# Gate and value layer by seven products: sums moved to GpSimd, bit operations issued one by one, buffers placed elsewhere

## The chip, the cores and the metric

One core of one Trainium2 chip. The metric is device time in microseconds (us). TensorE is PE in the profile (its weight loads PEld), VectorE DVE, ScalarE ACT, GpSimd POOL, and SyncE, which issues nearly all DMAs, SP.

## The reference

```python
q_assign = argmax(norm(q) . norm(centroids)); k_assign = argmax(norm(k) . norm(centroids))
scores = where(q_assign == k_assign, q k^T / 8, -1e9)      # 2 batches, 8 heads, 768 x 64
x = concat_heads(softmax(scores) v)                        # 1536 x 512
h = sigmoid(x @ w_gate) * (x @ w_val)                      # 512 x 1536 each, float64 weights
y = h @ w_out                                              # 1536 x 512, float64
p = domain_probs / sum(domain_probs)
out = sum over 4 experts e of p[:, e] * (relu(y @ w1[e]) @ w2[e])     # 512 x 1024 x 512
```

## The kernel before, in words

Every fp32 operand of a matmul is split into a rounded high part and the low rest (ACT copies the high part, POOL or DVE subtracts), and each product is three matmuls: high-high, high-low, low-high. Work goes in three stages: attention; the gate, value and output layer (`moe1`); four experts (`moe2`).

**Attention** runs 96 items of 128 queries. Per item PE computes scores and transposes, DVE takes the row maximum (L430) and the low parts (L451), ACT the exponential and the high parts. The table `TAIL` hangs the first weights of `moe1` into the last 12 items.

**Weights** arrive as 64-bit words. Per half of a unit (256 rows by 256 columns of the gate or value matrix, one p) `magnitude` runs two operations on ACT, `bits` three on DVE (L632 to L634), `rounded` one on POOL (L638). Then `sums` (L668) makes four sums of blocks and `split` four slices of high (ACT, L676) and low part (POOL, L677). Output weights (`outer`, 128 rows) go the same way in one piece: magnitude, bits, round, `woh` (L730), `wol` (L731).

**`seven`** multiplies a 2 x 2 block of weights with a 2 x 2 block of X by seven products instead of eight, in the order 1, 6, 7, 5, 2, 4, 3, six matmuls each, in four PSUM banks: bank 0 holds product 1 and then 2, bank 1 product 6 and then 4, bank 2 product 7, bank 3 product 5 and then 3. ACT copies product 1 to `m1`, DVE adds u2 = m1 + P6 (L768), u3 = u2 + P7 (L772), bank 2 = u3 + P5 (L776, Pn being product n), bank 1 = u3 - P4 (L782), bank 3 = u2 + P3 (L786). `evict` empties a bank: for `gate` by a sigmoid on ACT (L822), for `value` by a product on DVE (L834), a copy on ACT (L835), a subtraction on POOL (L836). Entries of the list `work` are issued by `side()` after each product: side steps 0 to 5.

**`outp`** multiplies `h` with `woh` and `wol`: 48 matmuls in eight groups of six, each group first with the even `outer` (f = 0) and then with the odd one (f = 1), in four PSUM banks; DVE adds each group to `acc` (L857; for p = 0 a copy, L855). One `work` entry follows each group.

**Order.** Every queue runs in the order of the code, arranged by hand. For p = 1 to 5 a period is gate(p, 0), outp(p-1, 1), value(p, 0), gate(p, 1), outp(p, 0), value(p, 1): 264 matmuls. The weights of the next unit are converted in `gate`, summed and split in `outp` and `value`; the odd `outer` is converted in gate(p, 1). For p = 0 the order is gate(0, 0), value(0, 0), outp(0, 0), gate(0, 1), value(0, 1), while the sums t1 to t4 of X for batch 1 (`right_operands`) and their seven splits are made. `raw` has two buffers, `rwo` one. At the end the operands of `moe2` for batch 0 are built (`operands`) beside outp(5, 1), and `hidden(0)`, `hidden(1)` are the first two `seven` calls of `moe2`.

Of the kernel before, what the change touches and what calls it, by code (L numbers as in the profile page):

```python
# [75 lines left out]
class Net:  # L76
# [459 lines left out]
    def attention(self):  # L536
# [146 lines left out]
    def unit(self, p, which):  # L683
# [108 lines left out]
    def moe1(self, xadd, xscale):  # L792
# [94 lines left out]
        def weights(u):  # L887
            return [[u["sums"]]] + [[go] for go in u["split"]]

        def dense(steps, n):  # L890
            out = [[] for _ in range(n)]
            for i, gos in enumerate(steps):
                out[i * n // len(steps)] += gos
            return out
# [5 lines left out]
        split0(1, nc.vector)  # L900
        split0(6, nc.gpsimd)
        gate(0, 0, [[vs[0], o0["mag"]], [lambda: split0(2, nc.vector), vs[1], o0["bits"]], [vs[2], o0["round"], o1["load"]],
                    [vs[3], o0["split"], sums["t1"]], [o1["mag"]], [o1["bits"], xadd, xscale]])
        for go in load(U[1][0]):
            go()
        value(0, 0, [[sums["t2"]], [o1["round"], sums["t3"]], [o1["split"], sums["t4"]],
                     [lambda: split(4, nc.vector)], [lambda: split(0, nc.vector)]])
        outp(0, 0, [[lambda: split(5, nc.vector)], [lambda: split(3, nc.gpsimd)], [lambda: split(1, nc.vector)],
                    [lambda: split(6, nc.gpsimd)], [lambda: split(2, nc.vector)]], soon=True)
        gate(0, 1, conv(U[1][0], 0) + conv(U[1][0], 1))  # L910
        value(0, 1, [load(U[1][1])] + weights(U[1][0]))
# [260 lines left out]
```

## Time and profile before

| | |
|---|---|
| median of 3 runs | 1133.11 us (1130.19 to 1134.36) |
| profiled execution | 1131.03 us, span 1129.2 us, mean granted clock 0.976 |
| busy, share of span | PE 1054.1 us (93%), DVE 859.4 (76%), POOL 597.6 (53%), ACT 541.1 (48%) |
| attention | up to 277.2 us |
| `moe1` | 277.2 to 609.9 us |
| end of `moe1`, start of `moe2` | 609.9 to 644 us |
| rest of `moe2` | 644 to 1129.2 us |

The profile tells, per engine, what was busy and what ended each wait. A granted clock of 1.00 is 2.4 GHz, 0.5 is 1.2 GHz.

### The profile page before, as it was taken

To read this page: it belongs to the slowest core of one execution; us is meant where nothing else is said; L and a number is where in the kernel's file an instruction comes from. 1 tells how busy PE (TensorE), PEld (TensorE's weight loads), DVE (VectorE), ACT (ScalarE), POOL (GpSimd) and SP (SyncE) were. 2 spreads that over 40 slices of the span, in tenths; PEclk is the share of its full clock that TensorE was granted. 3 is DMA by queue.
4 is the path that set the end of the run, shared out by engine and by line. 5 is a ranking of instruction groups with operands and counts; after the bars stand their busy time and mean duration, and the time that the engine had idled before them with its cause. 6 is when DMAs were issued, how large, how long until landed. Compare 5 with 4: busy or idle time off the path is not lost.

```text
span 1129.2 us, 16200 instructions
## 1 busy us (share of the span) xinstructions
PE 1054.1 (93%) x5813; PEld 976.1 (86%) x5813; DVE 859.4 (76%) x1472; ACT 541.1 (48%) x1138; POOL 597.6 (53%) x519
## 2 busy tenths in 40 slices
PE   6999999997688898988989799999999999999998
PEld 6998999996588898888979799889998989998897
DVE  6998889897777677867766787777668877667765
ACT  4887888886444343434333443333334333333330
POOL 7566567766446455545454664444445454444430
PEclk8999999999799899999999899999999999999999
DMA  7667787643111111112110212222112422122201
GB/s 169 144 161 163 158 175 158 144 123 99 56 56 57 57 56 57 56 56 73 57 45 33 75 61 71 75 75 76 63 49 63 143 75 75 42 71 76 75 19 57
DMA packets 86481, 95.87 MB, mean 85 GB/s; under 512 B 42720, under 2 KB 59456, under 8 KB 86400
## 3 DMA queue, kind: packets, MB, share of 16 engines
q1 hardware_dynamic: 85968, 94.77, 31.0%
q8 instruction: 46, 0.75, 0.3%
q14 instruction: 35, 0.29, 0.1%
q10 hardware_dynamic: 432, 0.06, 0.0%
HBM read 65.07 MB, written 3.19 MB: 60 GB/s over the span
## 4 chain that ended last, share of the span: by engine, by line
PE 48%; DVE 2%; issue 1%; POOL 1%; ACT 0%; POOLq 0%; DVEq 0%; ACTq 0%
PE ph L755 22%; PE po L1047 8%; PE po L1048 8%; PE po L1046 8%; DVE sf L668 1%; PE po L645 1%; PE po L643 1%; PE po L644 1%; POOL G L836 0%; DVE sg L834 0%; DVE acc L857 0%; DVE ph L782 0%; DVE h2l L1023 0%; POOL nq L969 0%; DVE ph L786 0%
## 5 line engine op out<-in xcount | busy, mean ns | idle before, releaser
L1003 POOL TENSOR_TENSOR wol<-r,woh 128x512 fp32r<-128x512 f32 x62 | 80.2, 1295 | 154.2 <-ACT woh L1002 154.1
L1053 DVE SCALAR_TENSOR_TENSOR acc<-po,pn,acc 128x512 f32<-128x512 f32 (+1 forms) x181 | 129.8, 742 | 36.2 <-PE po L1048 36.2
L677 POOL TENSOR_TENSOR w1l<-sf,w1h 128x512 fp32r<-128x512 f32 x88 | 114.7, 1319 | 67.9 <-ACT w1h L676 67.9
L1048 PE MATMUL po<-woh,h2l 128*128 128x512 f32 (+1 forms) x374 | 145.7, 389 | 0.0
L1047 PE MATMUL po<-wol,h2h 128*128 128x512 f32 (+1 forms) x374 | 145.6, 389 | 0.0
L1046 PE MATMUL po<-woh,h2h 128*128 128x512 f32 (+1 forms) x374 | 145.0, 388 | 0.0
L755 PE MATMUL ph<-h,w1h 128*128 128x384 f32 x336 | 116.3, 346 | 16.1 <-DVE ph L776 6.5
L1022 ACT ACTIVATE h2h<-ph 128x384 fp32r<-128x384 f32 x128 | 62.6, 490 | 113.8 <-PE ph L755 88.2
L755 PE MATMUL ph<-h,w1l 128*128 128x384 f32 x336 | 115.0, 342 | 0.3 <-POOL w1l L677 0.3
L755 PE MATMUL ph<-l,w1h 128*128 128x384 f32 x336 | 114.6, 341 | 0.0
L451 DVE TENSOR_TENSOR pl<-T,ph 128x384 fp32r<-128x384 f32 x192 | 97.4, 548 | 13.7 <-ACT ph L450 11.3
L676 ACT ACTIVATE w1h<-sf 128x512 fp32r<-128x512 f32 x88 | 55.6, 633 | 91.0 <-DVE sf L668 89.9
L1023 DVE SCALAR_TENSOR_TENSOR h2l<-ph,h2h 128x384 fp32r<-128x384 f32 x128 | 70.9, 554 | 36.0 <-ACT h2h L1022 32.8
L450 ACT ACTIVATE ph<-T 128x384 fp32r<-128x384 f32 x192 | 84.5, 493 | 19.4 <-PE T L447 18.9
L643 PE MATMUL po<-G,woh 128*128 128x384 f32 x192 | 70.6, 368 | 24.0 <-ACT woh L730 12.0
L430 DVE TENSOR_REDUCE nm<-S 128x1 f32<-128x768 f32 x96 | 91.0, 948 | 2.3 <-PE S L427 1.3
L427 PE MATMUL S<-R,L 80*128 80x384 f32 (+1 forms) x384 | 91.6, 361 | 0.3 <-ACT P L438 0.3
L447 PE MATMUL T<-ident,P 128*128 128x128 f32 x576 | 82.1, 276 | 8.3 <-DVE pl L451 7.9
L438 ACT ACTIVATE P<-S,nm 128x768 f32<-128x768 f32 x96 | 87.7, 914 | 3.1 <-DVE nm L430 3.1
L677 POOL TENSOR_TENSOR w1l<-r,w1h 128x512 fp32r<-128x512 f32 x64 | 68.0, 1065 | 36.8 <-ACT w1h L676 36.8
L755 PEld LDWEIGHTS ph<-h,w1h 128*128 128x128 f32 x336 | 64.5, 192 | 21.5 <-issue 5.6
L1048 PEld LDWEIGHTS po<-woh,h2l 128*128 128x128 f32 x374 | 70.2, 188 | 14.5
(260 smaller groups left out, 2860.9 us busy)
## 6 DMA issues: line engine op xcount, KB each, us to landing
r<-in_moe_w_dram SPq DMA_DIRECT2D x64, 512.0 KB, 3.7
L<-hiq SPq DMA_DIRECT2D x32, 192.0 KB, 5.0
R<-hik SPq DMA_DIRECT2D x32, 192.0 KB, 4.6
raw<-in_moe_w_gate_dram SPq DMA_DIRECT2D x12, 512.0 KB, 3.9
raw<-in_moe_w_val_dram SPq DMA_DIRECT2D x12, 512.0 KB, 3.8
rwo<-in_moe_w_out_dram SPq DMA_DIRECT2D x12, 512.0 KB, 4.5
nq<-in_q_dram SPq DMA_DIRECT2D x16, 192.0 KB, 3.8
nk<-in_k_dram SPq DMA_DIRECT2D x16, 192.0 KB, 3.9
```

The costliest lines, as they stand in the source:

```text
L427: nc.tensor.matmul(ps[:, a, 0:384], l[0:k, c], r[0:k, a * 384:a * 384 + 384], start=l is L1, stop=l is L2)
L430: nc.vector.tensor_reduce(nm, ps[:, :, 0:384], axis=AX.XY, op=ALU.max, negate=True)
L438: nc.scalar.activation(r2(pt), ps[:, :, 0:384], AF.Exp, bias=nm, scale=1.0, accum_out=P["sums"][:, i:i + 1])
L447: nc.tensor.transpose(ps[:, j, :], pt[:, c:c + 128], self.ident)
L450: nc.scalar.activation(hi, ps, AF.Copy)
L451: nc.vector.tensor_tensor(lo, ps, hi.bitcast(F32), op=ALU.subtract)
L677: nc.gpsimd.tensor_tensor(lo[:, sl], x, hi[:, sl].bitcast(F32), op=ALU.subtract)
L755: nc.tensor.matmul(ps, x[:, a, j], y[:, j], start=first and j == 0 and k == 0, stop=j == 1 and k == 2, skip_group_check=not first)
L1046: nc.tensor.matmul(ps, Hh[:, f, c], wh[:, dc], start=f == 0, stop=False)
L1047: nc.tensor.matmul(ps, Hh[:, f, c], wl[:, dc], start=False, stop=False)
L1048: nc.tensor.matmul(ps, Hl[:, f, c], wh[:, dc], start=False, stop=f == 1)
L1053: nc.vector.scalar_tensor_tensor(a, ps, pe, a, op0=ALU.mult, op1=ALU.add)
```

## The change

`TAIL` moves the first unit's steps one item earlier. A sigmoid of one element after the last items of attention loads the sigmoid's table there. `bits` becomes three separate steps, so that the lists of `moe1` put one DVE operation after each product. Sums of weights (in `moe1`) and of X (t1 to t4 of batch 1, and of batch 0 for `moe2`) go from DVE to POOL. With `early`, bank 2 is emptied straight behind the addition of P5. For p = 0 the copies to `acc` go from DVE to ACT. The odd `outer` is loaded behind outp(p-1, 1) and converted from side step 0 of gate(p, 1), the even one in outp(p-1, 1). The first odd `outer` takes a `raw` buffer, so on SP its load and one load of the next gate unit stand ahead of the last transfers of attention (rd, rb, the last A and W). The pools `qk`, `pp`, `sm` of attention are allocated first, and `tmp`, `wb` before `accp`, so `m1`, u2, u3 lie where scores' operands were, not on `U`.

```diff
 TAIL = {
-    "open": (-12, 2), "load00": (-12, 2), "load01": (-11, 0),
-    "mag00": (-9, 2), "bits00": (-8, 1), ... "bits01": (-7, 1), ... "sums0": (-6, 2),
+    "open": (-12, 0), "load00": (-12, 0), "load01": (-12, 0),
+    "mag00": (-10, 2), "bits00": (-9, 1), ... "bits01": (-8, 1), ... "sums0": (-7, 2),
...
         for _, g in pvs:
             list(g)
+            self.nc.scalar.activation(self.warm1, self.half[:, 0:1], AF.Sigmoid)
...
     def bits(self, raw, f):
+        return [lambda: ..., lambda: ..., lambda: ...]
...
     def seven(self, w, ops, temps, evict, work=(), early=False):
         nc.vector.tensor_tensor(p7, u3, p5, op=ALU.add)
+        if early:
+            evict(1, 1, p7)
+            side()
         product(2, p1, first=False)
         evict(0, 0, p1)
         side()
         p4 = bank(1)
         product(4, p4)
         nc.vector.tensor_tensor(p4, u3, p4, op=ALU.subtract)
-        evict(1, 1, p7)
+        if not early:
+            evict(1, 1, p7)
         side()
...
-        sums, split = self.right_operands(1, spare, temp, nc.vector)
+        sums, split = self.right_operands(1, spare, temp, nc.gpsimd)
...
                 if p == 0:
-                    nc.vector.tensor_copy(a, ps)
+                    nc.scalar.activation(a, ps, AF.Copy)
...
+        def conv(u, a=None):
+            args = () if a is None else (a,)
+            return [[lambda: u["mag"](*args)]] + [[lambda k=k: u["bits"](*args, (k,))] for k in range(3)] + \
+                [[lambda: u["round"](*args)]]
+        def total(u):
+            return [lambda: u["sums"](Q)]
...
+        value(0, 0, [[sums["t2"]], [go[0]] + d[0], d[1] + [sums["t3"]], d[2], d[3] + d[4], [sums["t4"], o1["split"]],
+                     [lambda: split(0, V), go[1]]])
...
         for p in range(1, NP):
-            o0["load"]()
-            gate(p, 0, conv(v, 0) + conv(v, 1))
-            outp(p - 1, 1, weights(v))
+            gate(p, 0, [c[0], c[1] + d[0], c[2], c[3] + c[4], d[1] + d[2], d[3] + d[4], total(v)])
...
-            value(p, 0, [[o0["mag"]], [o0["bits"]], [o0["round"]], [o1["load"], o0["split"]]])
-            gate(p, 1, (first or [[]] * 3) + [[o1["mag"]], [o1["bits"]], [o1["round"], o1["split"]]])
-            outp(p, 0, second + w[:-2])
+            c = conv(o0)
+            outp(p - 1, 1, [[vs[0]], [vs[1]], [vs[2]] + c[0], [vs[3]] + c[1], c[2], c[3], c[4]])
+            o1["load"]()
+            value(p, 0, [[], [o0["split"]]])
+            e = conv(o1)
             if p + 1 < NP:
-                value(p, 1, [load(U[p + 1][1])] + w[-2:])
+                gate(p, 1, [e[0], e[1], e[2], e[3] + e[4], [o1["split"]] + c[0], c[1] + c[2], c[3] + c[4]])
+                outers[2 * p + 2]["load"]()
+                outp(p, 0, [d[0], d[1], d[2], d[3] + d[4], total(g), [split[0]], [], [split[1]]])
+                value(p, 1, [load(U[p + 1][1]), [split[2]], [split[3]]])
...
-        sums = [lambda o=o, x=x, z=z: nc.vector.tensor_tensor(o, x, z, op=ALU.subtract)
+        add = nc.gpsimd if b == 0 else nc.vector
+        sums = [lambda o=o, x=x, z=z: add.tensor_tensor(o, x, z, op=ALU.subtract)
...
+        self.tmp = self.pool(es, "tmp")
+        self.wp.append(self.pool(es, "wb"))
         self.accp = self.pool(es, "accp")
```

Three places show what moves. First POOL in value(0, 0), before (co, wol: output weights; G: low part of h; k, W: splits of X; tB, tA, cv: the sums t1 to t4 of X).

```order
L638 TENSOR_TENSOR co<-co,rwo 128x512
L677 TENSOR_TENSOR w1l<-cv,w1h 128x256
L731 TENSOR_TENSOR wol<-co,woh 128x512
L638 TENSOR_TENSOR co<-co,rwo 128x512
L731 TENSOR_TENSOR wol<-co,woh 128x512
L836 TENSOR_TENSOR G_4224<-sg,G_4224 128x384 x4
L532 TENSOR_TENSOR k_4339<-tB,g_4338 128x768
L532 TENSOR_TENSOR W<-cv,A 128x768
```

The same place on POOL after the change.

```order
L641 TENSOR_TENSOR co<-co,rwo 128x512
L737 TENSOR_TENSOR wol<-co,woh 128x512
L520 TENSOR_TENSOR tA<-R_62,tB 128x768
L520 TENSOR_TENSOR cv<-tA,R_62 128x768
L846 TENSOR_TENSOR G_4214<-sg,G_4214 128x384 x2
L641 TENSOR_TENSOR co<-co,raw 128x512
L520 TENSOR_TENSOR cv<-tA,R_62 128x768
L737 TENSOR_TENSOR wol<-co,woh 128x512
L846 TENSOR_TENSOR G_4214<-sg,G_4214 128x384 x2
```

Three sums of X now stand among the low parts of h, and the odd `wol` stands behind two of these. Second, DVE in gate(1, 1) and the first groups of outp(1, 0), before (cv: a half of the next unit, co: the odd output weights).

```order
L768 TENSOR_TENSOR u_4799<-m_4798,ph_4812 128x384
L632 TENSOR_SCALAR cv<-cv 128x512
L633 TENSOR_SCALAR cv<-cv 128x512
L634 SCALAR_TENSOR_TENSOR cv<-raw,cv 128x512
L772 TENSOR_TENSOR u_4800<-u_4799,ph_4823 128x384
L776 TENSOR_TENSOR ph_4823<-u_4800,ph_4832 128x384
L782 TENSOR_TENSOR ph_4852<-u_4800,ph_4852 128x384
L632 TENSOR_SCALAR co<-co 128x512
L633 TENSOR_SCALAR co<-co 128x512
L634 SCALAR_TENSOR_TENSOR co<-rwo,co 128x512
L786 TENSOR_TENSOR ph_4832<-u_4799,ph_4832 128x384
L857 TENSOR_TENSOR acc_4111<-acc_4111,po 128x384 x2
```

The same place after the change.

```order
L774 TENSOR_TENSOR u_4801<-m_4800,ph_4816 128x384
L634 TENSOR_SCALAR co<-co 128x512
L778 TENSOR_TENSOR u_4802<-u_4801,ph_4825 128x384
L635 TENSOR_SCALAR co<-co 128x512
L782 TENSOR_TENSOR ph_4825<-u_4802,ph_4834 128x384
L636 SCALAR_TENSOR_TENSOR co<-rwo,co 128x512
L791 TENSOR_TENSOR ph_4857<-u_4802,ph_4857 128x384
L634 TENSOR_SCALAR cv<-cv 128x512
L635 TENSOR_SCALAR cv<-cv 128x512
L796 TENSOR_TENSOR ph_4834<-u_4801,ph_4834 128x384
L636 SCALAR_TENSOR_TENSOR cv<-raw,cv 128x512
L867 TENSOR_TENSOR acc_4115<-acc_4115,po 128x384 x2
```

The odd output weights come first and alternate with the additions. Third, POOL from gate(1, 1) to value(1, 1), after the change (before, no L668 stands on POOL here; those four stand on DVE between two additions to `acc`).

```order
L641 TENSOR_TENSOR co<-co,rwo 128x512
L737 TENSOR_TENSOR wol<-co,woh 128x512
L641 TENSOR_TENSOR cv<-cv,raw 128x512 x2
L671 TENSOR_TENSOR sf<-cv 128x256
L671 TENSOR_TENSOR sf<-sf,cv 128x256
L671 TENSOR_TENSOR sf<-cv 128x256
L671 TENSOR_TENSOR sf<-cv,sf 128x256
L680 TENSOR_TENSOR w1l<-cv,w1h 128x512
L680 TENSOR_TENSOR w1l<-sf,w1h 128x512 x2
L680 TENSOR_TENSOR w1l<-cv,w1h 128x256
L846 TENSOR_TENSOR G_4961<-sg,G_4961 128x384 x4
```

The four sums stand between the rounding of the two halves and the slices.

## Rows read from the trace of the kernel before

**Rows 1.** Busy time by stretch: start:end, length, PE, PEld, DVE, ACT, POOL (instructions), PEclk, DMA share, GB/s.
```profile
249.00:277.20 28.20, 21.00 (x124) 19.19 (x123) 23.47 (x38) 20.83 (x46) 18.88 (x18) 0.94 0.39 108
277.20:322.40 45.20, 29.35 (x127) 26.18 (x126) 30.70 (x38) 19.11 (x32) 21.43 (x15) 0.81 0.16 52
322.40:354.40 32.00, 28.68 (x158) 26.80 (x156) 25.92 (x46) 14.82 (x30) 17.14 (x14) 1.00 0.27 83
354.40:609.90 255.50, 232.81 (x1249) 223.52 (x1249) 183.10 (x324) 98.77 (x194) 130.84 (x112) 0.96 0.18 55
609.90:644.00 34.10, 26.70 (x133) 24.19 (x132) 25.05 (x37) 14.23 (x27) 21.33 (x17) 0.90 0.17 54
644.00:1129.20 485.20, 482.07 (x2420) 435.59 (x2418) 351.42 (x596) 169.38 (x337) 218.75 (x181) 1.00 0.21 69
```
**Rows 2.** The chain that ended last: start, us, engine, tile, line, instructions merged.
```profile
652.39 7.30 PE ph L755 x42
```
**Rows 3.** Waits of PE, 277.2 to 644 us: total us, times, longest.
```profile
PE po L643 <- ACT woh L730: 12.0, 5, 2.8
PE ph L755 <- DVE ph L776: 8.5, 8, 5.1
PE po L643 <- DVE acc L857: 6.3, 4, 1.6
PE po L645 <- POOL wol L731: 2.9, 5, 0.7
```
**Rows 4.** Timeline of DVE, 249 to 290 us: start, us, instruction [idle before].
```profile
255.01 1.91 DVE L633 TENSOR_SCALAR cv<-cv 128x512 int32<-128x512 int32 x1
...
289.61 0.56 DVE L776 TENSOR_TENSOR ph<-u,ph 128x384 f32<-128x384 f32 x1
```
**Rows 5.** Timeline of POOL, 249 to 306 us.
```profile
254.79 1.85 POOL L502 TENSOR_TENSOR A<-A,W 128x768 f32<-128x768 f32 x1 [1.00 <-DMA A<-U]
...
260.84 0.72 POOL L668 TENSOR_TENSOR sf<-cv 128x256 f32<-128x256 f32 x1
...
305.37 1.01 POOL L836 TENSOR_TENSOR G<-sg,G 128x384 fp32r<-128x384 f32 x1 [5.04 <-ACT G L835]
```
**Rows 6.** Timeline of ACT, 277 to 287 us.
```profile
277.48 0.49 ACT L467 ACTIVATE U<-PV 128x384 f32<-128x384 f32 x1 [2.46 <-PE PV L461]
277.87 0.84 ACT L529 ACTIVATE h<-R 128x768 fp32r<-128x768 f32 x1
...
281.61 0.49 ACT L764 ACTIVATE m<-ph 128x384 f32<-128x384 f32 x1 [2.17 <-DMA A<-U]
...
285.52 1.28 ACT L822 ACT_TABLE_LOAD   x1
```
**Rows 7.** Timeline of DVE, 451 to 460 us (gate(3, 0) and outp(2, 1)).
```profile
451.31 0.43 DVE L633 TENSOR_SCALAR cv<-cv 128x512 int32<-128x512 int32 x1
...
457.96 0.42 DVE L668 TENSOR_TENSOR sf<-sf,cv 128x256 f32<-128x256 f32 x1
458.31 1.52 DVE L668 TENSOR_TENSOR sf<-cv 128x256 f32<-128x256 f32 x1
```
**Rows 8.** Timeline of POOL, 458 to 461 us (outp(2, 1), slices of the weights).
```profile
458.22 1.32 POOL L677 TENSOR_TENSOR w1l<-cv,w1h 128x512 fp32r<-128x512 f32 x1 [0.75 <-ACT w1h L676]
459.50 1.46 POOL L677 TENSOR_TENSOR w1l<-sf,w1h 128x512 fp32r<-128x512 f32 x1
```
**Rows 9.** Timelines, 472 to 485 us (gate(3, 1) from its first matmul, outp(3, 0)).
```profile
472.29 0.33 PE L755 MATMUL ph<-g,w1h 128*128 128x384 f32 x1
...
475.50 0.66 DVE L632 TENSOR_SCALAR cv<-cv 128x512 f32<-128x512 f32 x1
...
480.47 0.69 DVE L634 SCALAR_TENSOR_TENSOR co<-rwo,co 128x512 int32<-128x512 int32 x1
...
482.70 0.63 ACT L730 ACTIVATE woh<-co 128x512 fp32r<-128x512 f32 x1 [0.55 <-POOL co L638]
...
483.41 1.29 POOL L731 TENSOR_TENSOR wol<-co,woh 128x512 fp32r<-128x512 f32 x1 [0.74 <-ACT woh L730]
```

More of the change, by code (lines that the diff above doesn't have):

```diff
@@ L579, in attention @@
         self.outers = [self.outer(f) for f in range(F1 // 128)]
-        tail = {"open": self.open_weights, "outer": self.outers[0]["load"]}
+        tail = {"open": self.open_weights, "outer0": self.outers[0]["load"], "outer1": lambda: self.outers[1]["load"](True)}
         for which in range(2):
@@ L699, in mag, with bits @@
             self.magnitude(raws[a], half(a))
-        def bits(a):
-            self.bits(raws[a], half(a))
+        def bits(a, steps=range(3)):
+            for k in steps:
+                self.bits(raws[a], half(a))[k]()
         def rounded(a):
@@ L712, in outer, with load @@
         nc, t = self.nc, {}
-        def load():
-            t["r"] = self.rwo.tile([128, 1, 512], I64, name="rwo", tag="rwo")
+        def load(spare=False):
+            t["r"] = self.raw.tile([128, 1, 512], I64, name="raw", tag="raw") if spare else \
+                self.rwo.tile([128, 1, 512], I64, name="rwo", tag="rwo")
             nc.sync.dma_start(out=t["r"][:, 0, :], in_=self.wo[f * 128:f * 128 + 128, :])
@@ L721, in mag, with bits @@
             self.magnitude(t["r"], t["f"])
-        def bits():
-            self.bits(t["r"], t["f"])
+        def bits(steps=range(3)):
+            for k in steps:
+                self.bits(t["r"], t["f"])[k]()
         def rounded():
@@ L879, in outp @@
                     go()
-        def conv(u, a):
-            return [[lambda: u["mag"](a)], [lambda: u["bits"](a)], [lambda: u["round"](a)]]
+        V, Q = nc.vector, nc.gpsimd
         def load(u):
             return [lambda: u["load"](0), lambda: u["load"](1)]
[L887 to L894, printed above, removed]
+        def conv(u, a=None):
[4 more added lines that the diff above has]
+            return [lambda: u["sums"](Q)]
         for p in range(1, NP):
@@ L899, in moe1 @@
         vs, o0, o1 = U[0][1]["split"], outers[0], outers[1]
[L900 to L911, printed above, removed]
+        c, d = conv(o0), conv(o1)
+        sums["t1"]()
+        split0(1, V)
+        gate(0, 0, [[lambda: split0(6, Q), vs[0]], [lambda: split0(2, V), vs[1]], c[0] + [vs[2]], c[1] + [vs[3]],
+                    c[2], c[3] + c[4], [xadd, xscale, o0["split"]]])
+        go = load(U[1][0])
+        value(0, 0, [[sums["t2"]], [go[0]] + d[0], d[1] + [sums["t3"]], d[2], d[3] + d[4], [sums["t4"], o1["split"]],
+                     [lambda: split(0, V), go[1]]])
+        outp(0, 0, [[lambda: split(4, V)], [lambda: split(5, V)], [lambda: split(3, V)], [lambda: split(1, V)],
+                    [lambda: split(6, Q)], [lambda: split(2, V)]], soon=True)
+        c, d = conv(U[1][0], 0), conv(U[1][0], 1)
+        gate(0, 1, [c[0], c[1], c[2], c[3] + c[4] + d[0], d[1] + d[2], d[3] + d[4], total(U[1][0])])
+        outers[2]["load"]()
+        value(0, 1, [load(U[1][1])] + [[go] for go in U[1][0]["split"]])
         for p in range(1, NP):
             v, (o0, o1) = U[p][1], outers[2 * p:2 * p + 2]
-            o0["load"]()
-            gate(p, 0, conv(v, 0) + conv(v, 1))
-            outp(p - 1, 1, weights(v))
+            c, d, vs = conv(v, 0), conv(v, 1), v["split"]
+            gate(p, 0, [c[0], c[1] + d[0], c[2], c[3] + c[4], d[1] + d[2], d[3] + d[4], total(v)])
             if p + 1 < NP:
@@ L920, in moe1 @@
                     go()
-                first, second = conv(g, 0), conv(g, 1)
-                w = weights(g)
             else:
@@ L1063, in moe2 @@
         sums, split = self.operands(1, [self.block(0, k, n) for k in range(2) for n in range(2)])
-        late = []
+        late = self.first_in
         for i in range(LAST):
```

50 lines of the change are left out of this document (24 added, 26 removed), and 10 rows, old and new, of the table TAIL.

## The prediction

> **What bounds the kernel now.** I read the busy time by stretch first [rows 1]. In the last 485 us PE is busy for 482.07: nothing is to be won there, and the change leaves it alone. A full-clock matmul of 384 columns takes 7.30 / 42 = 0.174 us of PE's path [rows 2]. Matmuls times 0.174 against the length gives what each stretch loses [rows 1]: 277.2 to 322.4 us (p = 0, batch 0) 45.2 - 127 x 0.174 = 23.1; the next 32.0 - 27.5 = 4.5; the five periods 255.5 - 217.3 = 38.2; the end 34.1 - 23.1 = 11.0. Together 76.8 us, in which alone the change can win, beside the tail of attention. Then the waits of PE say who ends them [rows 3]: the odd output weights (woh 12.0 and wol 2.9, once a period, in outp(p, 0)), the addition into bank 2 (L776, 8.5), the additions to `acc` (6.3 in four waits of 1.6). The reader is to see that DVE and POOL deliver late, though DVE stands idle for 72 of the 255.5 us [rows 1].
>
> Why they are late shows in single rows. L633 takes 0.43 alone and 1.91 when L502 of 1.85 runs on POOL [rows 4, 5, 7]; a sum of weights on DVE takes 0.42 alone and 1.52 when the slice w1l of 1.32 starts [rows 7, 8]. So a DVE operation on SBUF operands waits until POOL's current instruction ends, and what stands behind it in DVE's queue waits too. The Trainium skill ("GPSIMD Engine Reference", section 1, Specifications) says that GpSimd shares its SBUF interfaces with VectorE, with contention for two-port modes and two SBUF inputs. The trace agrees, with 0.42 against 1.52 us.
>
> **Tail of attention.** DVE bounds it: 23.47 of 28.2 us busy [rows 1]. Four halves cost 0.43 + 0.43 + 0.69 each alone [rows 7, 9], and one lost another 1.5 to L502 [rows 4]. One item earlier, the first two halves should meet an idle POOL, while the last two still meet slices of 1.3. I take a gain of 1.5, between 0 (all is lost again to POOL) and 4.
>
> **p = 0, batch 0.** The m1 copy stood 2.17 us behind the landing of A<-U, because m1 lay on U; then came a table load of 1.28 [rows 6]. Both leave the path: the table is loaded where ACT had 2.46 idle [rows 6], and m1 waits for ACT alone. On SP two loads now stand before the last A, W, rd and rb and wait for POOL's rounding of the value unit. They cost nothing while that rounding ends before the data of these transfers is there, which is its order today; if not, xadd and t2 move by as much. Chain, durations from [rows 4 to 6]: U copied at 278.0, h of R at 278.9, m1 at 279.3; DVE's low part (768 columns, some 1.0 after 0.42 for 256 [rows 7]) to 279.9, u2 0.5; ACT splits tA and one slice (1.3) and a second h, 281.4; DVE's low part, held by POOL's l (1.85), 283.0; u3, bank 2 at 284.1. Product 3 then starts at 284.1 instead of 290.2, when L776 ended before [rows 4]. In value(0, 0) product 1 (P1 for short) waits 0.4 for the sigmoid of bank 0, P6 0.9 for bank 1 (P4's subtraction stands behind two bits operations, each held by a slice of 1.3), P4 and P3 1.0 and 1.3 (u2 and bank 2 stand behind xadd and xscale): end near 296.0. outp(0, 0) then meets the new order on POOL: three sums of X of 1.85 [rows 5] lie among the four low parts G of 1.01. The first G comes near 298.2 (wait 2.2), the third, behind a sum, a rounding and wol, near 303.7 (wait 3.2); copies to `acc`, which share ACT with splits of 0.84, cost 1.3. End 296.0 + 2.2 + 3.2 + 1.3 + 48 x 0.174 = 311.0, against 322.4; 1 more for half clock behind the longer waits. Gain 10.5; between 5 (nothing is kept beyond product 3) and 17 (the G are not held by sums).
>
> **Next 32 us.** The `acc` wait there goes (the sums leave DVE), and the slices of U[1] come one side step earlier; one slice may still be 0.6 late. Lost 1.5 instead of 4.5: gain 3, between 1 and 4.5.
>
> **Five periods.** (a) Odd output weights: before, the last bits step ended at 480.47 + 0.69, 8.9 after the gate's first matmul (472.29), then came rounding, woh and wol [rows 9]. From the end of that step woh ends 2.17 and wol 3.54 later. Now: the first step ends 3.9 in, as L632 did there (475.50 + 0.66), u3 4.4, second step 4.9, bank 2 5.4, third step 6.1, so woh 8.3, wol 9.6. PE asks for woh 7.5 + 3 x 0.174 = 8.0 in, for wol 0.35 after it has woh: 0.3 and 1.0, with what refills the pipe 1.5 left of 3.0 (14.9 / 5) [rows 3]. Bank 2 is needed 6.4 in: 1.0 to spare. (b) The sums leave DVE: 1.6 a period gone [rows 3]; an addition from PSUM takes 0.56 [rows 4], and there are four banks. (c) On POOL a sum costs 0.72 [rows 5], four 2.9 a unit. In gate(p, 0) POOL rounds the second half until 10.9, sums until 13.8, slices until 15.1, 16.4, 17.7, 18.4; value(p, 0) starts at 15.65 and asks for them at 16.0, 17.05, 18.1, 20.9: covered by 0.4 to 2.5. If that cover goes, each value pays. (d) The loads of `outer` now follow the roundings that free `rwo`; they have half a period to land. (e) A clock of 0.96 over 255.5 us is worth 10.2 us [rows 1]; with shorter waits I expect 2 lost. What is left: 5 x 1.5, some 4 of small waits (bank 1 at the start of each gate is freed as late as before), 2 of clock: 13.5 instead of 38.2. Gain 25; between 8 (the `acc` waits and little else) and 33 (woh in time, no half clock).
>
> **End.** Sums for `moe2` go to POOL, but the sums for hidden(1) stay on DVE between u2 and u3 of hidden(0), each held by a slice (four took 0.42 to 1.52 [rows 7]); the slices then come late for hidden(1). I count waits of 0.3, 1.4, 2.3 and 3, and 1.5 of clock: 8.5 lost instead of 11.0; gain 2, between -3 and 6.
>
> **Sum.** 1.5 + 10.5 + 3 + 25 + 2 = 42 us. The profiled execution took 1131.0, 2.1 under the median of 1133.1: 1131.0 - 42 = **1089 us**. All lower ends give 1120, all upper ends 1066.
>
> **Rivals.** *POOL late* (16%): POOL's work in the periods, 130.84 us, grows by ten units of 2.9 to 160 of some 231, and its instructions stretch beside DVE (1.46 for 1.32 [rows 8]). Two us late per period break the cover of (c) in every value and gate: 10 x 1.7 = 17 lost, 1106. For: margins of 0.4. Against: POOL is idle half the time now. The Trainium skill ("GPSIMD Engine Reference", 4.1 Engine selection) would leave such additions on VectorE, GpSimd being about twice as slow with two inputs. By that factor, an estimate, four sums would take 3.4 us where the rows give 2.9, and the smallest cover in (c) would just be gone. The rows show 0.72 against 0.42, but also 1.52 for VectorE at this place [rows 5, 7].
>
> *Odd weights in time* (20%): if the first step meets no G on POOL, woh comes 1 us earlier, waits and half clock go: 5 x 1.5 + 2 less, 1079 or below.
>
> *Slower* (3%): POOL becomes the bound. Its 32 us a period (160 / 5) would have to stretch by 1.4 to 45, with 10 or more of waits for ACT and DVE (0.74 before wol alone [rows 9]): 55 instead of 231 / 5 = 46. Since 255.5 / 5 = 51.1 is today's period, it decides from 51 on: 5 x 4 lost against 17 won elsewhere, and with the same delay in p = 0, batch 0 (10 more) 1144. Against: the largest stretch in the rows is 1.46 / 1.32.
>
> *No effect* (2%): the waits named are not what holds PE, and others of equal size stand behind them: 1131. Against: four different waits at fixed places make up 30 of the 38.
>
> **Numbers.** The forecast has 59%. A measurement of this kernel tells a difference over 0.5% (5.7 us) from none. Range 1075 to 1107: it takes in the forecast, POOL late, and most of the odd weights in time. Faster 0.95, same 0.02, slower 0.03.
>
> **What would show it.** Right: no PE wait on `acc`; woh and wol waits of 1.5 a period; no m1 wait on A<-U and no table load between matmuls; outp(0, 0) ends near 309 to 311, behind waits on G; periods of 48 to 49 us; clock near 0.98 there. Wrong: w1l waits at the start of each value; L782 (L791 after the change) many us behind P4; POOL busy without a break through a period.

## The result, and the profile after

The changed kernel takes 1086.49 us (median of 4 runs, 1085.97 to 1089.09) against 1131.65 us (4 runs, 1129.47 to 1134.36), a ratio of 0.9604 (95% interval 0.9576 to 0.9633). The profiled execution took 1086.53 us, 44.5 less than that of before; the forecast was 42 less, and 1089.

Busy time by stretch after the change. The first six rows answer to [rows 1]; each ends at the same matmul as there (within one). The seventh goes from the 89th row maximum (L430) to the end of attention, the last covers 8 us of it.

```profile
249.00:278.36 29.36, 23.93 (x126) 21.21 (x125) 23.29 (x38) 22.62 (x50) 19.20 (x18) 0.83 0.47 126
278.36:312.96 34.60, 27.38 (x128) 24.82 (x128) 23.76 (x29) 19.43 (x37) 24.06 (x17) 0.90 0.15 46
312.96:341.50 28.54, 28.10 (x159) 27.27 (x159) 19.93 (x32) 16.71 (x35) 20.93 (x20) 1.00 0.22 60
341.50:570.90 229.40, 222.24 (x1249) 215.12 (x1247) 164.79 (x285) 104.20 (x204) 163.26 (x155) 1.00 0.21 67
570.90:599.44 28.54, 24.69 (x132) 22.53 (x133) 20.73 (x33) 12.67 (x24) 21.38 (x16) 1.00 0.12 38
...
599.44:1084.70 485.26, 482.04 (x2419) 435.55 (x2418) 351.24 (x596) 169.15 (x337) 217.72 (x181) 1.00 0.21 69
...
245.75:278.36 32.61, 27.18 (x149) 24.38 (x148) 26.36 (x43) 25.57 (x57) 19.58 (x19) 0.84 0.45 120
...
266.70:274.70 8.00, 7.23 (x27) 6.47 (x28) 6.50 (x13) 3.65 (x8) 5.72 (x7) 0.50 0.74 166
```

Against [rows 1] attention ends 1.2 later (278.36 against 277.20), p = 0, batch 0 is 10.6 shorter, the next stretch 3.5, the periods 26.1, the end 5.6, the rest 0.1 longer: 44.5 together. In the periods the granted clock rose from 0.96 to 1.00, and POOL works 163 of 229 us, as was counted (160 of 231).

Waits of PE after the change, 278.36 to 599.5 us (total, times, longest), to be laid beside [rows 3]:

```profile
PE ph L761 <- DVE ph L782: 4.8, 4, 1.5
PE po L648 <- POOL wol L737: 3.7, 5, 0.7
PE po L647 <- POOL G L846: 3.6, 3, 2.0
...
PE po L646 <- ACT acc L865: 1.2, 1, 1.2
...
PE po L646 <- DVE acc L867: 0.3, 1, 0.3
...
PE po L646 <- ACT woh L736: 0.2, 1, 0.2
```

The 12.0 us on woh are 0.2, the 6.3 on `acc` 0.3, the 8.5 on the addition into bank 2 are 4.8. What is left of the large stall is wol, 0.7 idle in each outp(p, 0) (the matmul starts 0.91 late).

Timeline of all engines after the change at three places: bits in the tail of attention; p = 0, batch 0 (the way to the first sigmoid in gate(0, 0), product 2 of value(0, 0), the third G of outp(0, 0)); and the odd output weights in gate(3, 1).

```profile
248.69 0.43 DVE L634 TENSOR_SCALAR cv<-cv 128x512 f32<-128x512 f32 x1
...
260.96 1.85 POOL L505 TENSOR_TENSOR R<-A,rb 128x768 f32<-128x768 f32 x1
261.80 1.29 DVE L634 TENSOR_SCALAR cv<-cv 128x512 f32<-128x512 f32 x1
262.77 2.86 POOL L680 TENSOR_TENSOR w1l<-sf,w1h 128x512 fp32r<-128x512 f32 x2
263.13 1.37 DVE L635 TENSOR_SCALAR cv<-cv 128x512 int32<-128x512 int32 x1
264.53 1.65 DVE L636 SCALAR_TENSOR_TENSOR cv<-raw,cv 128x512 int32<-128x512 int32 x1
...
266.70 0.69 PE L447 MATMUL T<-ident,P 128*128 128x128 f32 x2 [3.44 <-ACT ph L450]
...
276.11 1.28 ACT L617 ACT_TABLE_LOAD   x1
...
279.77 0.48 ACT L770 ACTIVATE m<-ph 128x384 f32<-128x384 f32 x1
...
285.01 0.41 PE L761 MATMUL ph<-h,w1h 128*128 128x384 f32 x1 [0.89 <-DVE ph L782]
...
290.92 0.63 ACT L736 ACTIVATE woh<-co 128x512 fp32r<-128x512 f32 x1 [1.61 <-POOL co L641]
...
291.98 0.45 PE L761 MATMUL ph<-h,w1h 128*128 128x384 f32 x1 [0.92 <-ACT m L770]
...
305.22 0.44 PE L647 MATMUL po<-G,woh 128*128 128x384 f32 x1 [2.03 <-POOL G L846]
...
448.67 0.33 PE L761 MATMUL ph<-g,w1h 128*128 128x384 f32 x1
...
453.99 0.68 DVE L636 SCALAR_TENSOR_TENSOR co<-rwo,co 128x512 int32<-128x512 int32 x1
...
456.23 0.63 ACT L736 ACTIVATE woh<-co 128x512 fp32r<-128x512 f32 x1 [1.19 <-POOL co L641]
...
456.91 0.44 PE L646 MATMUL po<-G,woh 128*128 128x384 f32 x1
456.94 1.29 POOL L737 TENSOR_TENSOR wol<-co,woh 128x512 fp32r<-128x512 f32 x1 [0.74 <-ACT woh L736]
...
458.28 0.44 PE L648 MATMUL po<-G,wol 128*128 128x384 f32 x1 [0.75 <-POOL wol L737]
```

In the tail the first halves find POOL idle (0.43), the third finds the addition of X and two slices: 1.29, 1.37 and 1.65 where 0.43, 0.43 and 0.69 would do. PE then stands for 3.44. In gate(0, 0) the table is loaded before attention's last copy, m1 no longer waits for a DMA [rows 6], and product 3 starts at 285.01, where before it stood until L776 ended at 290.2 [rows 4]. In value(0, 0) product 2 (291.98) waits for the bank that m1's copy frees, and this copy stands on ACT behind woh, which waits 1.61 for POOL's rounding. In gate(3, 1) woh is ready 8.2 after the first matmul (456.86 - 448.67) and asked for at about 8.1 (the first f = 1 matmul at 456.91 has a gap of 0.1 before it); wol is ready at 9.6.

### The profile page after: what moved, and what is told of

Same layout as the page of the kernel before. It is cut to its first block, busy times and chain, and to the rows that moved or that the text cites. A ratio compares the mean times of both kernels' runs of the same rounds, so it can differ in the third digit from the quotient of the medians.

```text
span 1084.7 us, 16243 instructions
## 1 busy us (share of the span) xinstructions
PE 1041.2 (96%) x5813; PEld 966.0 (89%) x5813; DVE 824.4 (76%) x1407; ACT 548.5 (51%) x1156; POOL 637.5 (59%) x568
## 3 DMA queue, kind: packets, MB, share of 16 engines
q1 hardware_dynamic: 85968, 94.77, 32.1%
## 4 chain that ended last, share of the span: by engine, by line
PE 80%; DVE 9%; POOL 3%; ACT 3%; issue 2%; DMA 2%; SPq 0%; POOLq 0%; DVEq 0%; ACTq 0%
PE ph L761 31%; PE po L1058 8%; PE po L1059 8%; PE po L1057 8%; PE T L447 5%; PE S L427 4%; PE po L648 3%; PE po L647 3%; PE po L646 2%; PE PV L460 2%; PE PV L461 2%; DVE nm L430 1%; DVE pl L451 1%; DMA R<-hik 1%; POOL co L641 1%
## 5 line engine op out<-in xcount | busy, mean ns | idle before, releaser
L761 PE MATMUL ph<-h,w1l 128*128 128x384 f32 x336 | 112.8, 336 | 0.7 <-POOL w1l L680 0.7
L430 DVE TENSOR_REDUCE nm<-S 128x1 f32<-128x768 f32 x96 | 91.1, 949 | 2.0 <-PE S L427 1.0
L1057 PEld LDWEIGHTS po<-woh,h2h 128*128 128x128 f32 x374 | 70.2, 188 | 13.9
L1058 PEld LDWEIGHTS po<-wol,h2h 128*128 128x128 f32 x374 | 70.2, 188 | 13.9
```

Of the source, the lines that this page charges most:

```text
L430: nc.vector.tensor_reduce(nm, ps[:, :, 0:384], axis=AX.XY, op=ALU.max, negate=True)
L761: nc.tensor.matmul(ps, x[:, a, j], y[:, j], start=first and j == 0 and k == 0, stop=j == 1 and k == 2, skip_group_check=not first)
L1057: nc.tensor.matmul(ps, Hh[:, f, c], wh[:, dc], start=f == 0, stop=False)
L1058: nc.tensor.matmul(ps, Hh[:, f, c], wl[:, dc], start=False, stop=False)
```

## The experiments

All ratios are to the kernel before, run again beside each experiment (medians of 1129.9 to 1132.3). The lengths are read from the traces, one execution each: tail (from the 89th row maximum to the end of attention), p = 0, batch 0 (to the end of outp(0, 0)), the periods (here from the first matmul of outp(0, 1) to that of outp(5, 1)) and the end (to the end of hidden(1)).

| | median us | ratio (95%) | tail | p=0, b=0 | periods | end |
|---|---|---|---|---|---|---|
| before | 1131.7 | 1 | 32.1 | 45.2 | 262.4 | 34.2 |
| after | 1086.5 | 0.960 (0.958 to 0.963) | 32.6 | 34.6 | 235.0 | 28.5 |
| e1 sums on VectorE | 1103.9 | 0.978 (0.974 to 0.981) | 32.6 | 34.6 | 253.9 | 28.5 |
| e2 odd weights last | 1111.7 | 0.984 (0.980 to 0.988) | 30.5 | 34.6 | 263.2 | 28.5 |
| e3 bits in a block | 1087.1 | 0.963 (0.959 to 0.967) | 30.6 | 37.0 | 232.1 | 28.5 |
| e4 X sums on VectorE | 1086.4 | 0.962 (0.958 to 0.965) | 30.2 | 35.0 | 234.7 | 28.6 |
| e5 m1 on U, no early table | 1090.5 | 0.965 (0.962 to 0.968) | 30.5 | 39.5 | 234.7 | 29.1 |
| e6 before, sums on GpSimd | 1124.5 | 0.995 (0.993 to 0.997) | 33.9 | 45.3 | 254.0 | 35.3 |
| e7 before, odd weights first | 1111.1 | 0.983 (0.979 to 0.986) | 33.4 | 45.4 | 239.7 | 34.9 |
| e8 odd weights sooner | 1084.1 | 0.959 (0.955 to 0.962) | 30.5 | 34.6 | 233.0 | 29.1 |
| e9 all | 1077.4 | 0.951 (0.948 to 0.955) | 32.6 | 34.5 | 222.5 | 25.8 |
| e10 e9 and the tail | 1072.4 | 0.946 (0.943 to 0.950) | 29.3 | 34.4 | 222.6 | 25.7 |
| e11 e10 and moe2's start | 1069.3 | 0.947 (0.944 to 0.950) | 29.3 | 34.5 | 222.7 | 25.7 |
| e12 end sums on VectorE | 1087.4 | 0.962 (0.960 to 0.965) | 32.2 | 34.7 | 234.6 | 30.2 |

**e1 and e6: who adds the weights.**

```diff
-            return [lambda: u["sums"](Q)]
+            return [lambda: u["sums"](V)]
```

> The four sums of weights of each unit in moe1 go back to VectorE, at the places in the order where GpSimd has them now. Theory (the sums held up the additions to acc): the waits of TensorE on acc come back at 1.6 us in each of the five outp(p, 1), and nothing else moves: 5 x 1.6 = 8 more, 1094 us, ratio to the kernel before 0.967. Rival (GpSimd is what is short now): without four sums of 0.72 per unit GpSimd rounds, slices and forms wol sooner, the wol waits of 0.91 a period shrink: 1082 to 1086. Second rival (it does not matter who adds, since four banks cover it): 1086.5, ratio 0.960.

Waits of PE in the periods of e1, 337.78 to 591.66 us:

```profile
PE po L646 <- DVE acc L867: 10.7, 4, 2.7
PE po L648 <- POOL wol L737: 3.7, 5, 0.7
```

The periods grow by 18.9, over twice what was expected: four waits of 2.7 instead of 1.6, the waits on wol not changed at all, and 0.97 granted clock instead of 1.00. The waits are longer than they were because the place is another: the sums now stand ahead of the first addition to `acc`, where before they stood behind it, and a group of six matmuls takes 1.04. The first theory held in kind, and both rivals fell. The counterpart makes the same move in the kernel before, where it is the only one:

```diff
-            return [[u["sums"]]] + [[go] for go in u["split"]]
+            return [[lambda: u["sums"](nc.gpsimd)]] + [[go] for go in u["split"]]
```

> The kernel before with one edit: the four sums of weights of each unit in moe1 go to GpSimd, at the same places. Theory (they hold up the additions to acc): the acc waits of 6.3 in the periods and 2.7 at p = 0 go, the woh waits stay: 1131 - 9 = 1122 us, ratio 0.992. Rival (GpSimd is late with the slices, since 2.9 us of sums stand ahead of four slices of 4.7 in outp(p - 1, 1), where 8.4 us are to be had): waits on w1l of 1 or more at the start of each value(p, 0), 1128 to 1135, ratio 1.0.

Waits of PE in the periods of e6, 346.13 to 600.13 us:

```profile
PE po L643 <- ACT woh L730: 12.0, 5, 2.8
```

The `acc` waits are gone, those on woh are the same as in [rows 3], and none on w1l came. The periods are 8.4 shorter in the trace; the medians differ by 5.4 (1124.5 against 1129.9).

**e2 and e7: the place of the odd output weights.**

```diff
-                gate(p, 1, [e[0], e[1], e[2], e[3] + e[4], [o1["split"]] + c[0], c[1] + c[2], c[3] + c[4]])
+                gate(p, 1, [c[0], c[1] + c[2] + c[3], c[4], [], e[0], e[1] + e[2] + e[3], e[4] + [o1["split"]]])
```

> In gate(p, 1) the odd output weights go back to the places they had in the kernel before: behind the half of the next unit, magnitude behind product 2, bits in one block behind product 4, rounding and split at the end. All else stays as after the change. Theory (the place of the odd weights made the largest stall of a period, and with it the half clock): woh waits of 2.4 and wol waits of 0.6 a period return as in the kernel before, against 0.91 now, and a stretch at half clock of 3.4 us or more, worth 1.7: 2.1 + 1.7 = 3.8 a period, 5 x 3.8 = 19, so 1105 us, ratio 0.977. Rival (the odd weights were late because sums and blocks stood in VectorE's way, which are gone): woh is in time at the old place too, 1087 to 1090.

Waits of PE in the periods of e2, 332.69 to 595.86 us:

```profile
PE po L646 <- ACT woh L736: 17.0, 5, 3.6
PE po L648 <- POOL wol L737: 2.8, 5, 0.7
```

28.2 us for one list put back, a little more than the 27.4 that the periods had gained (with `early` a `seven` has seven side steps, so the list has seven entries; it also puts the bits back in a block, which e3 shows to cost nothing in the periods). The waits on woh are even longer than the 12.0 of [rows 3], and the granted clock is 0.94. In gate(3, 1) the wait is 3.56 where it was 2.31: PE asks 0.4 sooner, and woh is ready 0.8 later (11.85 after the first matmul against 11.04), because on ACT its magnitude now stands behind the early eviction of bank 2, which waits 2.80 for L782. The same place changed in the kernel before, alone:

```diff
-            gate(p, 1, (first or [[]] * 3) + [[o1["mag"]], [o1["bits"]], [o1["round"], o1["split"]]])
+            gate(p, 1, [[o1["mag"]], [o1["bits"]], [o1["round"], o1["split"]]] + first)
```

> The kernel before with one edit: in gate(p, 1) the odd output weights are converted in the first three side steps and the half of the next unit in the last three. Theory (their place made the stall): woh is ready three products (3.1 us) sooner, the woh waits of 12.0 and most of the wol waits of 2.9 go, and with them the 20.5 us at half clock in the periods that follow these waits, worth 7: 1131 - 18 = 1113 us, ratio 0.984. Rival (VectorE is late in all, and the next unit's half takes the place of the odd weights): the waits come back on the slices of the next gate or on acc, 1123 to 1131, ratio 0.993 to 1.0.

Waits of PE in the periods of e7, 352.26 to 591.92 us:

```profile
PE po L643 <- DVE acc L857: 6.2, 4, 1.6
...
PE po L645 <- POOL wol L731: 1.2, 5, 0.2
```

No wait on woh is left, the waits on `acc` are those of before, and the clock is 1.00. This edit alone takes 22.7 us off the periods (18.9 off the median); the whole change takes 27.4 off them.

**e3: one by one or in a block.**

```diff
-            return [[lambda: u["mag"](*args)]] + [[lambda k=k: u["bits"](*args, (k,))] for k in range(3)] + \
+            return [[lambda: u["mag"](*args)], [lambda: u["bits"](*args)], [], []] + \
```

> The three bit operations of each half again stand together, where the first of them stands now; rounding keeps its place. Theory (issued one by one they fit between the additions): u3 or bank 2 now stands behind 0.43 + 0.43 + 0.69 = 1.55 us instead of at most 0.69, and behind 1.3 more where GpSimd holds one: waits on bank 2 (L782) of 0.3 to 1 in two of the four seven calls of a period, 5 x 1 to 2, so 1092 to 1097 us. Rival (VectorE has a product's time of 1.04 us to spare at each addition, and it is the early place that counts): no wait on L782 above 0.3, 1086.5 within 2.

Timeline of e3, value(0, 0):

```profile
291.70 1.17 DVE L634 TENSOR_SCALAR co<-co 128x512 f32<-128x512 f32 x1
292.67 1.86 POOL L520 TENSOR_TENSOR cv<-tA,R 128x768 f32<-128x768 f32 x1
292.91 1.91 DVE L635 TENSOR_SCALAR co<-co 128x512 int32<-128x512 int32 x1
294.85 0.69 DVE L636 SCALAR_TENSOR_TENSOR co<-raw,co 128x512 int32<-128x512 int32 x1
295.46 0.56 DVE L782 TENSOR_TENSOR ph<-u,ph 128x384 f32<-128x384 f32 x1
...
296.07 0.69 PE L761 MATMUL ph<-h,w1h 128*128 128x384 f32 x1 [3.56 <-DVE ph L782]
```

Both were right, each in its place. (L634, L635 and L636 are the block, L782 the addition into bank 2 behind it.) For p = 0, where POOL runs 1.85 us sums, bank 2 stands behind a block of 3.8 us and PE waits 3.56: the stretch loses 2.4, and gate(0, 1) to gate(1, 0) another 1.6. The periods are 2.9 shorter with the block; 1.2 of it is the wait on the `acc` copy in outp(0, 1), which goes. The total is the same, as the rival said, though by a loss and a gain that cancel.

**e4: the sums of X.**

```diff
-        sums, split = self.right_operands(1, spare, temp, nc.gpsimd)
+        sums, split = self.right_operands(1, spare, temp, nc.vector)
```

> The sums t1 to t4 of X for batch 1 go back to VectorE at the places where GpSimd has them now. Theory (they stand in the way of the low parts G on GpSimd): the wait of 2.2 us on the third G in outp(0, 0) and the half clock behind it go, and VectorE pays three sums of about 1 us each in value(0, 0), part of it covered: the stretch from the end of attention to the end of outp(0, 0) falls from 34.6 to about 32.5, 1084.5 us. Rival (VectorE is the bound of value(0, 0), and each sum is held by a slice on GpSimd of 1.3): product 3 and the last evictions come 3 to 5 later, stretch 38, 1090 us.

Neither: 0.4 longer, at a granted clock of 0.85 in the stretch against 0.90, so the sign of this difference is open. The matmul behind the third G starts 1.09 late instead of 2.20, but the one behind the second G (the first that outp(0, 0) asks for) 1.51 instead of 1.07, and u2 of value(0, 0) stands 1.91 behind t2, which costs 1.11.

**e5: m1 on U, and the table.** The pools are allocated in the order of the kernel before, and:

```diff
-            self.nc.scalar.activation(self.warm1, self.half[:, 0:1], AF.Sigmoid)
```

> The order of the pools of the kernel before returns, so that m1, u2 and u3 lie on U again, and the sigmoid of one element after the last items of attention is taken out. Theory (both stood on the path of p = 0, batch 0): the first m1 waits for the landing of A<-U, some 2.7 us after its issue at 279.1, and is 2.0 later than the 279.8 of the changed kernel; the table load of 1.28 again stands in front of the first eviction of a bank by a sigmoid; the stretch from the end of attention to the end of outp(0, 0) grows from 34.6 by 3.3 to 38, 1090 us. Rival (the waits on G in outp(0, 0) come from GpSimd's own order and end at the same moment, so the delay is swallowed): stretch 34.6 to 35.5, 1087 us, with smaller waits on G.

Timeline of e5 (the code is one line shorter than after the change):

```profile
277.27 0.52 SPq L474 DMA_DIRECT2D A<-U  x1
277.84 0.60 SPq L475 DMA_DIRECT2D W<-U  x1
282.51 0.49 ACT L769 ACTIVATE m<-ph 128x384 f32<-128x384 f32 x1 [5.40 <-DMA W<-U]
...
287.16 1.28 ACT L831 ACT_TABLE_LOAD   x1
```

The stretch is 4.9 longer. The copy waits for both transfers from U, and starts 4.7 after the second is issued (before, it waited 2.17 [rows 6]); the table load stands in the path as forecast. What each of the two costs by itself was not tried.

**e8: the odd weights sooner.**

```diff
-            value(p, 0, [[], [o0["split"]]])
+            value(p, 0, [[], [o0["split"]], [], [], [], e[0]])
-                gate(p, 1, [e[0], e[1], e[2], e[3] + e[4], [o1["split"]] + c[0], c[1] + c[2], c[3] + c[4]])
+                gate(p, 1, [e[1], e[2], e[3] + e[4], [o1["split"]], c[0], c[1] + c[2], c[3] + c[4]])
```

> The changed kernel with the odd output weights one step sooner still: the magnitude in side step 5 of value(p, 0), the bit operations in steps 0 to 2 of gate(p, 1), the split in step 3. Theory (wol comes 0.91 late in each outp(p, 0), the whole of the rest of the large stall): the five waits go, 5 x 0.91 = 4.5: 1082 us, ratio 0.956. Rival (co has one buffer: the magnitude waits on ACT until GpSimd has formed the even wol from it, and the sigmoids or copies behind it are late): 0 to 5 slower, 1087 to 1091, with waits on sg or m1 in gate(p, 1).

Only 2.0 of the 4.5. In four of the five periods the magnitude, asked for sooner, waits for the load of the odd weights (3.3 us in all, 1.84 in gate(3, 1)). There it and two G copies stand ahead of m1 on ACT, so the second and third bits operation, which stand behind u2 and u3, hardly come sooner. The waits on wol fell from 3.7 to 1.9.

**e9, e10, e11: what is left.** e9 puts the bits of a half in a block for p > 0, the odd magnitude in step 4 of value(p, 0), and more:

```diff
+                gate(p, 1, [e[1] + e[4], [o1["split"]], [], [], c[0], c[1], c[4]])
...
+        if early:
+            evict(1, 0, p4)
...
-        value(NP - 1, 1, [..., [lambda: ysplit(0, V), ys[1]], [lambda: ysplit(1, V)], []])
+        value(NP - 1, 1, [..., [lambda: ysplit(0, V), ys[1]], [], [], [], [], [lambda: ysplit(1, V)]])
-                         ..., [cin[0], cin[1]]], soon=True)
+                         ..., [lambda: cin[0](Q), cin[1]]], soon=True)
...
+            hidden(i, late + w if i == 0 else w + late)
```

> The changed kernel with what the runs so far point to. In the periods the bit operations of a half in one block (one by one only for p = 0); the odd magnitude in side step 4 of value(p, 0), its bits and rounding in step 0 of gate(p, 1), its split in step 1; bank 1 emptied straight behind the subtraction of P4, ahead of product 3; at the end the low part of y21 behind the evictions of value(5, 1), the sums for hidden(1) on GpSimd, and the slices of hidden(1) ahead of the second output weights. Theory (the waits left in the trace of the changed kernel are what is left to win): wol 5 x 0.91 = 4.5, the acc copy 1.3, bank 1 9 x 0.23 = 2.1, the end 1.65 + 1.40 + 0.80 + 0.89 = 4.7; of these 12.6 some 10 stay: 1076 us, ratio 0.952. Rival (each wait taken away shows the next one behind it, a few tenths shorter): 1082 us or more, ratio 0.957.

A period takes 45.8 instead of 47.7, which is 264 matmuls of 0.1734 and nothing else. In the periods 12.5 are won and at the end 2.7, together 15 where some 10 were expected; 6.4 are lost behind it: outp(0) of `moe2` waits for additions that stand behind a late DMA, and half clock follows. That 1077.4 is so near the 1076 of the forecast is luck. e10 moves three slices in the tail:

```diff
-    "split00": (-7, 2), "split01": (-6, 2), "mag10": (-5, 2), "split02": (-5, 2), "bits10": (-4, 1), ...
-    "split03": (-4, 2), ...
+    "split00": (-7, 2), "mag10": (-5, 2), "bits10": (-4, 1), "round10": (-4, 1), "split01": (-4, 2),
+    ... "split02": (-3, 2), "split03": (-3, 2),
```

> The kernel of e9 with one more edit, in the tail of attention: the second, third and fourth slice of the first gate unit on ACT and GpSimd stand behind the bit operations of the first half of the value unit, not ahead of them. Theory (each of these three bit operations waited for a slice on GpSimd, 4.3 us instead of 1.55, TensorE stood still for 3.4 and fell to half clock): the stretch from the 89th row maximum (item 88) to the end of attention, 30.5 to 32.6 us in the runs of the changed kernel's tail, falls to 28 to 29, and the whole by 2 against e9. Rival (the slices, later, are missed by the first products of gate(0, 0), or the last half meets them instead): the stretch and the waits behind it together stay at 30.5 or more, no difference to e9.

Timeline of e10, the third half in the tail (lines one higher):

```profile
262.09 1.68 DVE L635 TENSOR_SCALAR cv<-cv 128x512 f32<-128x512 f32 x1
263.81 0.43 DVE L636 TENSOR_SCALAR cv<-cv 128x512 int32<-128x512 int32 x1
264.27 0.69 DVE L637 SCALAR_TENSOR_TENSOR cv<-raw,cv 128x512 int32<-128x512 int32 x1
...
265.49 0.55 PE L448 MATMUL T<-ident,P 128*128 128x128 f32 x3 [1.64 <-DVE pl L452]
```

Without the slices two of the three operations take their own time, and PE stands for 1.64 instead of 3.44. The tail takes 29.3, against 32.6 in e9 and 30.2 to 32.6 in all nine kernels with the tail of the changed one. e11 then mends what e9 broke:

```diff
-            hidden(i, late + w if i == 0 else w + late)
+            hidden(i, late + w if i < 2 else w + late)
-                late = cin
+                late = [lambda go=cin[0]: go(nc.gpsimd)] + cin[1:] if i == 0 else cin
```

> The kernel of e10 with one more edit at the start of moe2. In e10 the second pair of output weights is formed after the slices of hidden(1), so its buffer is free 3.9 us later, the next load lands later, and ACT waits 6.3 us for it in hidden(1) with the evictions of hidden(1) behind it; outp(0) of moe2 then waits 3.5 on acc and 1.9 of half clock follow. Edit: in hidden(1) too the slices of the next weights stand ahead of the output weights, and their four sums go to GpSimd. Theory: that wait and the half clock go: 1072.4 - 5 = 1067.5 us, ratio 0.943. Rival (the output weights, later still, are then missed by outp(1), or the sums on GpSimd hold up hidden(1)): 1072 or more, ratio 0.947.

Busy time by stretch of e11, the periods and the rest of `moe2`:

```profile
333.61:556.31 222.70, 222.20 (x1279) 221.22 (x1278) 169.14 (x289) 105.71 (x208) 168.44 (x158) 1.00 0.24 72
...
582.03:1067.60 485.57, 482.29 (x2419) 435.51 (x2418) 350.92 (x592) 169.69 (x338) 221.06 (x184) 1.00 0.21 71
```

PE is busy for 222.20 of 222.70. The rest of `moe2`, 490.2 in e10, is back at 485.6, and the median is 3.1 lower; but the ratios, each to its own runs of the kernel before, are 0.946 and 0.947. That e11 beats e10 is told by the trace, not by the times.

**e12: the end.**

```diff
-        add = nc.gpsimd if b == 0 else nc.vector
+        add = nc.vector
```

> The changed kernel, with the sums t1 to t4 for moe2 (batch 0) back on VectorE. The stretch from the start of outp(5, 1) to the end of hidden(1) took 34.15 us before and takes 28.5 after the change, a gain of 5.6 where 2 were forecast. Theory (these sums of 768 columns, 1.84 to 2.57 us each on GpSimd, were what VectorE was short of at the end): the stretch grows to 31 to 34, and value(5, 1) loses 1 to 2 as well: 1091 us, ratio 0.965. Rival (the gain comes from the new order of splits and of the sums for hidden(1) in the lists, not from who adds): stretch 28 to 29.5, 1087 us, ratio 0.962.

30.2, between the two: sums on GpSimd are worth 1.7 there (part of it half clock: 0.94 granted against 1.00). The other 3.9 come from the rest of the change; that it is the new order of the lists, as the rival has it, was not tried alone. The stretch ahead of it, with value(5, 1), gained 0.4 instead of losing.

## Why the prediction was right, step by step

- **The bound.** The change could win only where PE waits, and 44.5 came from there; the last 485 us did not move. That the sum is only 2.5 off is in part luck: a tail 2.0 short of its gain stands against an end 3.6 over it.
- **Tail: right at like clock, not in this execution.** A gain of 1.5 was forecast, and 0.5 was lost (32.61 against 32.06), at a granted clock of 0.84 against 0.95. All nine kernels with the changed tail have the same stall in it, and they took 30.2 to 30.6 at 0.94 to 1.00 (e2, e3, e4, e5, e8), 32.2 at 0.89 (e12) and 32.6 at 0.84 (e1, e9 and the changed kernel). With the old tail it is 32.1 at 0.95, 33.4 at 0.90 (e7) and 33.9 at 0.85 (e6): at like clock the change gains 1.2 to 1.6. What differs is the clock behind the stall (last section). The first two halves met an idle POOL as forecast. "The last two still meet slices of 1.3" was wrong in kind: the third met an addition of X and two slices in a row and took 2.8 longer than alone, the fourth only 0.3.
- **p = 0, batch 0: right, 10.6 for 10.5, with other waits inside.** Product 3 of gate(0, 0) comes 6.65 after the end of attention where it came 13.0 after it; the chain gave 6.1 of these 6.4. e5 puts m1 on U and the table back: 4.9. That is not 2.17 + 1.28 because m1 there waits 5.40, for the later of two transfers; before, it waited 2.17 for the first. The waits in value(0, 0) were 0.40, 1.08 and 1.32 (starts of matmuls) where 0.4, 0.9, 1.0 and 1.3 stood; that of 1.08 was not in the forecast, which had its 1.0 at P4 behind xadd and xscale: it is at product 2, behind m1's copy and woh. In outp(0, 0) the wait on the third G was 2.2 (3.2 forecast), on the first that PE asks for 1.35 for its high part and 1.07 for its low one (2.2), on copies to `acc` nothing (1.3); some 20 matmuls 0.32 apart instead of 0.174 cost 2.9 (1). The bits one by one hold 2.4 of the gain (e3).
- **Next 32 us: right.** 28.54 - 158 x 0.174 = 1.0 lost, where 1.5 stood.
- **Five periods: right in the sum, 26.1 for 25; the odd weights are worth more than their step gave them.** The times of that step hold to 0.1: woh ready 8.2 in, wol 9.6 in (8.3 and 9.6 forecast). But the 1.5 left a period were 0.9, and with the waits on woh all half clock went, not 8 of 10.2. Other waits make 5.1 where some 4 stood: 2.1 on bank 1 (9 x 0.23), 1.3 on the copy to `acc` in outp(0, 1), 1.65 on bank 2 in value(5, 1). The rival *odd weights in time* was half true: woh in time, wol not. Moved alone, the odd weights gave 22.7 and the sums 8.4, together 31.1 against the 27.4 that both and all else gave (e7, with the odd bits in a block, has 1.2 of waits on wol where the changed kernel has 3.7); undone alone, they cost 28.2 and 18.9. A sum of terms hides this: undone alone, each stall comes back larger than it was (waits of 17.0 for 12.0 and 10.7 for 6.3), and with half clock behind it (0.94 and 0.97). The waits of 1.6 on `acc` that e7 leaves bring none (1.00).
- **POOL late: fell.** No wait on w1l in the periods, though the smallest cover was 0.4. The Trainium skill ("GPSIMD Engine Reference", 4.1 Engine selection) would have left the sums on VectorE. Here e1 and e6 show 18.9 and 8.4 us in favour of GpSimd.
- **End: right in sign, 5.6 for 2.** The largest wait before was of PE on the evictions of hidden(0), behind the slices and the sums for hidden(1):

```profile
PE ph L755 <- DVE h2l L1023: 4.4, 1, 4.4
```

That wait is gone. The terms "1.4, 2.3 and 3" were too large: three of the four sums for hidden(1) took 1.48 to 1.56 before, and they were to stay "each held by a slice"; now the four took 1.46, 1.04, 0.41 and 0.41 on DVE, since POOL stood idle beside the last two (586.7 to 587.7). The waits were 1.2 idle on bank 2, 0.6 and 0.7 on slices, and there was no half clock.

Not tried alone were `early`, the copies to `acc` on ACT, the earlier loads, and the new `TAIL`; what each is worth stays open.

## What to carry to other kernels

Ask of each stall when its product is ready and when it is asked for, counted from the same matmul: that step held to 0.1 us and carried most of the gain in the periods. Move work to a slower engine where the slower one has cover and the faster one has a queue that others wait for. In this kernel, an order in which single operations are interleaved was worth something only where the other engine held long instructions against them (e3: 4.0 us won for p = 0, 2.9 lost in the periods).

## What the runs showed that was not expected

The same stall was followed by different clocks. After PE's idle of 3.44 in the tail the changed kernel had half clock for the next 8 us; e2, with the same instructions there and 3.42 idle, had this (busy time by stretch of e2, the 8 us from the same matmul, and the whole tail):

```profile
265.50:273.50 8.00, 7.09 (x36) 6.12 (x37) 6.72 (x13) 4.64 (x11) 5.80 (x7) 0.83 0.65 181
...
244.59:275.10 30.51, 25.01 (x148) 22.16 (x147) 26.37 (x43) 25.45 (x57) 19.63 (x19) 0.94 0.41 121
```

From the stalled matmul to the end of attention it is 11.66 us in the changed kernel and 9.60 in e2: that is the 2.1 us between 30.51 and 32.61. So two executions with the same stall can differ by 2 us, and a difference of that size in a stretch with a stall is not yet the work of an edit while the granted clocks differ. With the shorter stall of 1.64 the tail was 29.3 both at 0.94 (e10) and at 1.00 (e11). Why the clock differs was not tried.

A DVE operation on SBUF operands waiting out POOL's instruction, told from 0.42 against 1.52 [rows 7], showed again: 1.65 for 0.69 in the tail, 1.91 for 0.43 in e3. The Trainium skill ("GPSIMD Engine Reference", section 1, Specifications) names the shared SBUF interfaces. The rows say that what counts is the length of the single instruction on GpSimd, 1.85 for a sum of X and 1.3 for a slice.
